# The norm's inverse root moved from eleven VectorE instructions to GpSimd's power, and taken per half in the first block

## The chip, the core and the metric

One NeuronCore of a Trainium2 chip runs the whole kernel. The metric is the device time of one execution in microseconds, given as the median over the runs of a kernel. Engines are named as in the profile: PE is TensorE (PEld its weight loads), DVE is VectorE, ACT is ScalarE, POOL is GpSimd, and SP is the engine that only issues transfers here.

## What is computed

The reference is an attention without softmax, a norm over the head dimension, and a gated feed-forward block:

```python
kv  = np.einsum('bhsd,bhse->bhde', k, v)          # 8 batches, 8 heads, 576 tokens, 64 wide
out = np.einsum('bhsd,bhde->bhse', q, kv)
rms = np.sqrt(np.mean(out * out, axis=-1, keepdims=True) + 1e-06)
x   = (out / rms * g_norm)                         # then (B,H,S,D) -> (4608, 512)
g   = x @ w_gate                                   # 512 -> 1536
silu = g * (1.0 / (1.0 + np.exp(-g)))
y   = (silu * (x @ w_val)) @ w_out                 # 1536 -> 512
```

The inputs reach the chip as 64-bit floats. Attention inputs are loaded through strided views, and the feed-forward weights are converted to float32 on the chip, from their two 32-bit words.

## The kernel before

The 4608 tokens are taken in nine blocks of 512 (`NB` = 9). A block has an attention part (class `Att`) and a feed-forward part (class `Ffn`). The attention part of block n + 1 is done inside the last stage of block n, so that TensorE always has products to work on. Block 0 has nobody to hide behind: its attention part is the method `first` (L466), and it is the start of the program.

The attention part of a block consists of these steps. `turn_q` transposes q. `heads` multiplies q with the kv matrix of each head into two PSUM tiles per half of the tokens. `squares` (L367) squares these tiles on ScalarE (L374) and sums them over the head dimension on VectorE (L375) into a small tile `z`: 128 partitions, and 32 values in each, 16 for each half of the tokens. `root` (L377) makes the inverse square root of the mean of squares plus epsilon. It does this on VectorE with one affine step (L381), a first guess from the bits of the number (L384) and three Newton steps of three instructions (L391 to L393): eleven instructions on 128x32 values. `scale` (L395) multiplies each PSUM tile with the root, broadcast over the head dimension, on VectorE (two instructions for each half, recorded at the helper's line L113). `turn_x` transposes the result on TensorE (L410), and ScalarE copies it with the gain (L411) to the tile `x`. From block 1 on, `whole` (L505) does both halves in one go, with one root for both, and the transposes are made by VectorE and transfers (`blocks_x`, `place_x`); `root` there is recorded after the second half's squares.

In `first`, both halves share one root as well: `heads` and `squares` of half 0, the products and squares of half 1, then `root(0, 2)`, `scale(0)`, the first weight piece, `turn_x(0)` and `scale(1)`. Between the products of half 1 and the transposes of half 0 stands `warm` (L492): seven float32 products of 128x512 that nobody reads, put in TensorE's queue.

Weights come in pieces of 512 KB. A piece is begun by `Words.begin` (ScalarE L146, then VectorE L147, L152 and L153) and finished by `Words.finish` (ScalarE L160, then VectorE L162). Block 0's feed-forward part (`plain_up`, L1032) needs one piece of `w_gate` and one of `w_val` for each of its 12 column groups; its first column group is split in two halves of the tokens, so that the first can begin when half 0 of x is there.

Three things order the work. Each engine has one queue and takes it in order. The program leaves the order to a scheduler, which follows priorities and the data; `tc.issue_after(...)` holds instructions back until another has been issued. Pools give the buffers: `st_pool` (two) for `z` and `y`, `r_pool` (five) for the large rings, PSUM pools `a` (one bank), `b` (three), `c` (two), `m` (two). GpSimd has no work until 105.78 us; later it has subtractions of weights (L112), some products and sums. Before each attention part of blocks 3 to 8 stand three subtractions of `turn_t(7)`, and three of `turn_t(4)` that wait for the scales (L1003).

Of the kernel before, what the change touches and what calls it, by code (L numbers as in the profile page):

```python
# [8 lines left out]
F32 = mybir.dt.float32  # L9
U32 = mybir.dt.uint32  # L10
I32 = mybir.dt.int32
OP = mybir.AluOpType
ACT = mybir.ActivationFunctionType

P = 128
# [3 lines left out]
def kernel(  # L19
# [41 lines left out]
    nc = tc.nc  # L61

    B, H, S, D = q.shape
# [7 lines left out]
    NS = DM // P  # L71
# [4 lines left out]
    eps = 1e-6  # L76
# [3 lines left out]
    def pool(name, bufs, **kw):  # L80
        return ctx.enter_context(tc.tile_pool(name=name, bufs=bufs, **kw))

    consts = pool("consts", 1)
    ld_pool = pool("ld", 4)
    st_pool = pool("st", 2)
# [8 lines left out]
    a_psum = pool("a_psum", 1, space=PS)  # L94
    b_psum = pool("b_psum", 3, space=PS)
# [6 lines left out]
    gain = consts.tile([P, 1], F32, name="gain")  # L102
    for u in range(2):
        nc.gpsimd.dma_start(out=gain[u * D : (u + 1) * D], in_=g_norm.rearrange("(d o) -> d o", o=1))

    kvs = [consts.tile([P, NS, D], F32, name=f"kv{i}") for i in range(3)]

# [11 lines left out]
    class Words:  # L119
# [12 lines left out]
        def __init__(self, src, shape):  # L132
            self.raw = ld_pool.tile([P, LD], U32, name="ld")[:, 0 : 2 * BLK]
            dst = self.raw.rearrange("p (a b) -> p a b", a=shape[0])
            self.sent = nc.sync.dma_start(out=dst, in_=src)
            self.shape = shape
            self.begun = False
# [45 lines left out]
    def round_w(name, j):  # L183
        if name == "o":
            dst = wo[:, j : j + 1, :]
        else:
            dst = wviews[name][0][j // 2][:, :, P * (j % 2) : P * (j % 2 + 1)]
        piece = words.pop((name, j))
        if not piece.begun:
            piece.begin()  # L190
        return piece.finish(dst)

    class Att:


        def __init__(self, n):
            self.n = n

            self.cut, half = divmod(n, 2)
            self.split = half * D  # L200
            self.ps, self.z = {}, None
            self.q, self.k, self.v, self.room = [], {}, {}, None
            self.halves = []
            self.quarters = n > 0

        def parts(self, t):

            n, first = self.n, P * t - D * self.n
            if t < self.cut:
                return [(n - 1, S + first, 0, P)]  # L210
            if t == self.cut and self.split:
                return [(n - 1, S - D, 0, D), (n, 0, D, P)]
            return [(n, first, 0, P)]
# [162 lines left out]

        def root(self, i, k=1):  # L377


            z = self.z[:, i : i + k]  # L380
            nc.vector.tensor_scalar(out=z, in0=z, scalar1=1.0 / D, scalar2=eps, op0=OP.mult, op1=OP.add)  # L381
            self.y, a = (st_pool.tile([P, 2, 2, 2, NS], F32, name=x) for x in "ya")
            y, a = self.y[:, i : i + k], a[:, i : i + k]
            nc.vector.tensor_scalar(  # L384
                out=y.bitcast(I32), in0=z.bitcast(I32), scalar1=-0.5, scalar2=float(0x5F3759DF),
                op0=OP.mult, op1=OP.add,
            )
            flat = lambda t: t.rearrange("p i u t j -> p (i u t j)")
            y, a, z = flat(y), flat(a), flat(z)
            for _ in range(3):  # L390
                nc.vector.scalar_tensor_tensor(out=a, in0=y, scalar=-0.5, in1=y, op0=OP.mult, op1=OP.mult)  # L391
                nc.vector.tensor_tensor(out=a, in0=a, in1=z, op=OP.mult)
                nc.vector.scalar_tensor_tensor(out=y, in0=a, scalar=1.5, in1=y, op0=OP.add, op1=OP.mult)  # L393

        def scale(self, i):  # L395
            if i == 0:
# [69 lines left out]
        def first(self):  # L466
            self.turn_q(0, (b_psum, c_psum))
            self.first_kv(0, (b_psum, c_psum))
            last = self.first_kv(1, (b_psum, a_psum))

            with tc.issue_after(last.ins):
                self.heads(0, (0, 1), (m_psum, m_psum))
            with tc.issue_after(self.multiplied.ins):
                self.heads(0, (2, 3))
            self.squares(0)
            with tc.issue_after(self.multiplied.ins):
                self.turn_q(1, (b_psum, c_psum))

            with tc.issue_after(self.copied_q.ins), tc.issue_after(self.summed.ins):
                begun = words[pieces[0]].begin()  # L480
            with tc.issue_after(begun.ins):
                self.product(1, (b_psum, a_psum))
            self.warm()
            self.root(0, 2)
            self.scale(0)
            with tc.issue_after(self.squared.ins), tc.issue_after(self.scaled.ins):
                weights(1)
            self.turn_x(0)
            self.scale(1)
            return self.squared, self.scaled  # L490

        def warm(self):  # L492

            ps = c_psum.tile([P, NS, P], F32, name="c")
            for _ in range(7):
                nc.tensor.matmul(ps, lhsT=ident, rhs=self.qt[:, 3], start=True, stop=True)

        def turn(self):
# [553 lines left out]
    def load_weights(upto):  # L1052
        nonlocal loaded, sent
        while loaded < min(upto, len(pieces)):
            load_w(*pieces[loaded])
            loaded += 1
            if loaded == len(pieces) - NP:
                sent = words[pieces[loaded - 1]].sent

    def weights(upto):  # L1060
        nonlocal rounded
        while rounded < min(upto, len(pieces)):
            load_weights(rounded + 4)
            round_w(*pieces[rounded])
            rounded += 1
# [106 lines left out]
```

## Time and profile before

| | |
|---|---|
| time, median of 3 runs | 1024.2 us (1023.02 to 1026.13) |
| span of the profiled execution | 1021.4 us |
| granted TensorE clock | 1.000 |
| first transposes of x (L410) | at 27.16 us |
| TensorE without gaps from | 33.72 us |
| one root on VectorE, block 0 | 2.47 us (23.26 to 25.73) |
| GpSimd's first instruction after the constants | at 105.78 us |

The profile is of one execution. A row of a timeline gives start, duration, engine, line of the kernel, operation, output<-inputs, shapes and count, and in brackets how long the engine had been idle before it and what it waited for. The page has the totals by engine, the busy share in 40 slices of the span (a digit is tenths), and the chain that ended last.

### The profile page before, as it was taken

Reading aid. Unit: us, or ns where it says so; the run is one execution under the profiler, and the core shown is the slowest. Engines: PE = TensorE matmul, PEld = TensorE weight load, DVE = VectorE, ACT = ScalarE, POOL = GpSimd, SP = SyncE. Lnnn points to the kernel's source line nnn. Section 1 sums busy time; section 2 is a strip of 40 time slices with the busy share of each in tenths; the row PEclk is TensorE's granted clock in tenths of the full one; section 3 lists DMA queues with packets and bytes.
Section 4 is the critical chain, followed back from the end, with each engine's and each line's share of the span. In section 5 each row is a group of like instructions: output and inputs, shape, how many; then the busy total and the mean of one; then the engine's idle time right before and its main releaser. Section 6 shows DMA issues by size and latency. Waiting matters only on the chain.

```text
span 1021.4 us, 21409 instructions
## 1 busy us (share of the span) xinstructions
PE 1006.0 (98%) x8522; PEld 897.1 (88%) x8522; DVE 701.1 (69%) x1169; ACT 227.9 (22%) x353; POOL 369.0 (36%) x280
## 2 busy tenths in 40 slices
PE   6999999999999999999999999999999999999998
PEld 4544688888999989998999899988998999989997
DVE  2999688998665946685558566665669466946661
ACT  2765112121211221121121211111121211221110
POOL 0000263534055503561246315630555045513670
PEclk9999999999999999999999999999999999999999
DMA  8689643767888377845686568636772766066601
GB/s 237 203 255 271 124 77 108 187 165 156 250 210 255 60 176 203 252 92 129 209 238 144 96 195 247 177 60 201 231 199 46 177 195 190 22 167 201 191 27 42
DMA packets 273845, 170.26 MB, mean 167 GB/s; under 512 B 150609, under 2 KB 241873, under 8 KB 273745
## 3 DMA queue, kind: packets, MB, share of 16 engines
q1 hardware_dynamic: 238800, 164.42, 59.3%
q10 hardware_dynamic: 34880, 4.46, 2.7%
q8 instruction: 68, 1.11, 0.4%
q14 instruction: 33, 0.26, 0.1%
q0 software_dynamic: 64, 0.00, 0.0%
HBM read 138.02 MB, written 22.41 MB: 157 GB/s over the span
## 4 chain that ended last, share of the span: by engine, by line
PE 90%; DVE 6%; DMA 2%; issue 1%; ACT 1%; SPq 0%; DVEq 0%; ACTq 0%
PE b L728 26%; PE b L565 19%; PE c L728 13%; PE c L565 10%; PE a L728 6%; PE a L565 5%; PE b L1032 4%; PE c L1032 4%; PE m L316 2%; PE m L361 1%; DVE r L112 1%; DVE xi L112 1%; DVE r L111 1%; DMA h<-in_v_dram 1%; DVE t L112 1%
## 5 line engine op out<-in xcount | busy, mean ns | idle before, releaser
L111 POOL TENSOR_TENSOR r<-r 128x256 f32<-128x256 f32 (+1 forms) x105 | 110.8, 1061 | 300.9 <-DVE r L111 272.2
L111 DVE TENSOR_TENSOR r<-b,r 128x512 f32<-128x512 f32 (+1 forms) x273 | 161.9, 606 | 65.5 <-PE b L728 60.1
L112 POOL TENSOR_TENSOR t<-wo 128x512 f32<-128x512 f32 x81 | 114.5, 1438 | 212.4 <-DVE wo L111 102.9
L111 DVE TENSOR_TENSOR r<-c,r 128x512 f32<-128x512 f32 (+1 forms) x179 | 108.5, 617 | 89.0 <-PE c L728 54.8
L728 PE MATMUL b<-x,t 128*128 128x128 f32 x1092 | 151.3, 276 | 0.0
L111 DVE TENSOR_TENSOR r<-a,r 128x512 f32<-128x512 f32 (+1 forms) x99 | 62.5, 631 | 113.4 <-PE a L565 70.7
L728 PEld LDWEIGHTS b<-x,t 128*128 128x128 f32 x1092 | 136.5, 192 | 0.8
L728 PE MATMUL c<-xi,t 128*128 128x128 f32 x840 | 112.4, 276 | 0.4 <-DVE xi L111 0.4
L113 POOL TENSOR_TENSOR h<-r 128x1024 f32<-128x1024 f32 (+1 forms) x40 | 82.3, 2072 | 76.9 <-DVE r L111 73.9
L728 PEld LDWEIGHTS c<-xi,t 128*128 128x128 f32 x840 | 102.9, 192 | 0.5 <-DVE xi L111 0.5
L565 PE MATMUL b<-wo,h 128*128 128x256 f32 x432 | 100.1, 383 | 0.1
L565 PE MATMUL b<-t,h 128*128 128x256 f32 x432 | 96.9, 381 | 0.0
L565 PEld LDWEIGHTS b<-t,h 128*128 128x128 f32 x432 | 81.6, 190 | 11.3 <-issue 0.2
L565 PEld LDWEIGHTS b<-wo,h 128*128 128x128 f32 x432 | 79.9, 190 | 13.1 <-DVE h L113 2.5
L742 ACT COPY r<-b 128x512 f32<-128x512 f32 x63 | 36.9, 585 | 211.6 <-PE b L728 211.6
L728 PE MATMUL b<-xi,t 128*128 128x128 f32 x588 | 79.8, 276 | 0.0
L728 PEld LDWEIGHTS b<-xi,t 128*128 128x128 f32 x588 | 72.4, 192 | 0.0
L728 PE MATMUL b<-x,wg 128*128 128x128 f32 x336 | 52.7, 279 | 0.2 <-DVE x L112 0.2
L728 PE MATMUL b<-x,wv 128*128 128x128 f32 x336 | 51.4, 276 | 0.0
L565 PE MATMUL a<-wo,h 128*128 128x256 f32 x216 | 48.3, 379 | 0.0
L565 PE MATMUL c<-t,s 128*128 128x256 f32 x216 | 48.1, 380 | 0.0
L565 PE MATMUL c<-wo,h 128*128 128x256 f32 x216 | 48.1, 379 | 0.0
(133 smaller groups left out, 1565.7 us busy)
## 6 DMA issues: line engine op xcount, KB each, us to landing
t<-w SPq DMA_DIRECT2D x336, 256.0 KB, 3.6
out_dram<-r SPq DMA_DIRECT2D x17, 512.0 KB, 3.1
ld<-in_k_dram SPq DMA_DIRECT2D x26, 288.0 KB, 5.2
ld<-in_v_dram SPq DMA_DIRECT2D x26, 288.0 KB, 5.9
ld<-in_moe_w_gate_dram SPq DMA_DIRECT2D x12, 512.0 KB, 4.8
ld<-in_moe_w_val_dram SPq DMA_DIRECT2D x12, 512.0 KB, 4.7
ld<-in_moe_w_out_dram SPq DMA_DIRECT2D x12, 512.0 KB, 4.9
w<-t SPq DMA_DIRECT2D x18, 256.0 KB, 3.0
```

The lines of the kernel that those rows point to most:

```text
L111: add = lambda e, o, a, b: e.tensor_tensor(out=o, in0=a, in1=b, op=OP.add)
L112: sub = lambda e, o, a, b: e.tensor_tensor(out=o, in0=a, in1=b, op=OP.subtract)
L113: mul = lambda e, o, a, b: e.tensor_tensor(out=o, in0=a, in1=b, op=OP.mult)
L316: nc.tensor.matmul(self.kv_ps[r][u * D : (u + 1) * D, g, :], lhsT=k[:, u, c, :], rhs=v[:, u, c, :], start=(c == 0), stop=(c == KT - 1),)
L361: self.multiplied = nc.tensor.matmul(self.ps[i][u][p : p + D, t, j, :], lhsT=self.qt[rows, 2 * i + t, j, p : p + D], rhs=kvs[b % 3][rows, ...
L565: nc.tensor.matmul(banks[e][:, e], lhsT=lhsT, rhs=rhs, start=first and i == 0 and (e == 0 or banks[0] is not banks[1]), stop=i == self.ste ...
L728: nc.tensor.matmul(ps[:, i, f], lhsT=self.weight(o, p, f), rhs=self.operand(o, p), start=first and (i, f) == (0, 0), stop=True, skip_group ...
L742: nc.scalar.copy(out=dst, in_=ps)
L1032: nc.tensor.matmul(t, lhsT=w[f // 2][:, i, P * (f % 2) : P * (f % 2 + 1)], rhs=x[:, i, of], start=(i == 0), stop=(i == NS - 1),)
```

## The change

The root is taken by GpSimd: one affine step and one power with the exponent -0.5 from a constant tile, in place of eleven instructions of VectorE, in all nine blocks. In block 0 each half of the tokens has a root of its own, so that half 0 can be scaled and transposed before half 1 is squared and summed; the beginning of the first weight piece is put between, and the squares of half 1 after the scale of half 0. The unused products go from seven to two. It is meant to take work off VectorE in the start of the program and to let TensorE begin with real work earlier.

```diff
+    half = consts.tile([P, 8 * NS], F32, name="half")
+    nc.gpsimd.memset(half, -0.5)
...
         def root(self, i, k=1):
-            z = self.z[:, i : i + k]
-            nc.vector.tensor_scalar(out=z, in0=z, scalar1=1.0 / D, scalar2=eps, op0=OP.mult, op1=OP.add)
-            self.y, a = (st_pool.tile([P, 2, 2, 2, NS], F32, name=x) for x in "ya")
-            y, a = self.y[:, i : i + k], a[:, i : i + k]
-            nc.vector.tensor_scalar(
-                out=y.bitcast(I32), in0=z.bitcast(I32), scalar1=-0.5, scalar2=float(0x5F3759DF),
-                op0=OP.mult, op1=OP.add,
-            )
-            flat = lambda t: t.rearrange("p i u t j -> p (i u t j)")
-            y, a, z = flat(y), flat(a), flat(z)
-            for _ in range(3):
-                nc.vector.scalar_tensor_tensor(out=a, in0=y, scalar=-0.5, in1=y, op0=OP.mult, op1=OP.mult)
-                nc.vector.tensor_tensor(out=a, in0=a, in1=z, op=OP.mult)
-                nc.vector.scalar_tensor_tensor(out=y, in0=a, scalar=1.5, in1=y, op0=OP.add, op1=OP.mult)
+            self.y = self.y or st_pool.tile([P, 2, 2, 2, NS], F32, name="y")
+            z, y = (x[:, i : i + k].rearrange("p i u t j -> p (i u t j)") for x in (self.z, self.y))
+            nc.gpsimd.tensor_scalar(out=z, in0=z, scalar1=1.0 / D, scalar2=eps, op0=OP.mult, op1=OP.add)
+            nc.gpsimd.tensor_tensor(out=y, in0=z, in1=half[:, 0 : 4 * NS * k], op=OP.pow)
...
             self.squares(0)
+            self.root(0)
             with tc.issue_after(self.multiplied.ins):
                 self.turn_q(1, (b_psum, c_psum))
 
             with tc.issue_after(self.copied_q.ins), tc.issue_after(self.summed.ins):
                 begun = words[pieces[0]].begin()
             with tc.issue_after(begun.ins):
-                self.product(1, (b_psum, a_psum))
+                self.scale(0)
+            first = self.scaled
+            with tc.issue_after(self.copied_q.ins):
+                self.heads(1, range(NS), (b_psum, a_psum))
             self.warm()
-            self.root(0, 2)
-            self.scale(0)
-            with tc.issue_after(self.squared.ins), tc.issue_after(self.scaled.ins):
+            with tc.issue_after(first.ins):
                 weights(1)
+                self.squares(1)
+            self.root(1)
             self.turn_x(0)
+            with tc.issue_after(self.squared.ins), tc.issue_after(self.summed.ins):
+                weights(2)
             self.scale(1)
             return self.squared, self.scaled
 
         def warm(self):
             ps = c_psum.tile([P, NS, P], F32, name="c")
-            for _ in range(7):
+            for _ in range(2):
                 nc.tensor.matmul(ps, lhsT=ident, rhs=self.qt[:, 3], start=True, stop=True)
```

More of the change, by code (lines that the diff above doesn't have):

```diff
@@ L200, in __init__ @@
             self.split = half * D
-            self.ps, self.z = {}, None
+            self.ps, self.z, self.y = {}, None, None
             self.q, self.k, self.v, self.room = [], {}, {}, None
```

## The prediction, made before the changed kernel was run

> **What bounds the kernel now.** I read the page first (engine totals, the 40 slices, the chain that ended last):
>
> ```profile
> PE 1006.0 (98%) x8522; PEld 897.1 (88%) x8522; DVE 701.1 (69%) x1169; ACT 227.9 (22%) x353; POOL 369.0 (36%) x280
> ...
> PE   6999999999999999999999999999999999999998
> ...
> PE 90%; DVE 6%; DMA 2%; issue 1%; ACT 1%; SPq 0%; DVEq 0%; ACTq 0%
> ```
>
> TensorE sets the end: it is full in every slice but the first, and 90% of the chain is its work. The waits of TensorE sum to 11.8 us, and 9.3 of them are for the first transfers. So time can only be gained where TensorE is busy with nothing useful, or cold. The timeline of TensorE between 20 and 36 us shows where (start, duration, engine, line; two records are one float32 matmul):
>
> ```profile
> 20.67 6.28 PE L496 MATMUL c<-r,ident 128*128 128x512 f32 x14
> 27.16 1.07 PE L410 MATMUL m<-ident,r 128*128 128x128 f32 x8 [0.21 <-DVE r L113]
> 28.57 1.99 PE L1032 MATMUL b<-x,wg 128*128 128x256 f32 x8 [0.34 <-ACT x L411]
> 30.40 0.93 PE L410 MATMUL m<-ident,r 128*128 128x128 f32 x7
> 31.41 1.99 PE L1032 MATMUL c<-x,wv 128*128 128x256 f32 x8
> 33.24 0.27 PE L410 MATMUL m<-ident,r 128*128 128x128 f32 x1
> 33.72 1.99 PE L1032 MATMUL b<-x,wg 128*128 128x256 f32 x8 [0.20 <-ACT x L411]
> ```
>
> The seven products of L496 are never read: they fill 20.67 to 26.95 while VectorE makes the root. From 33.72 on TensorE has no gap worth naming. VectorE in the same stretch (timeline of DVE):
>
> ```profile
> 21.96 1.27 DVE L375 TENSOR_REDUCE z<-r 128x8 f32<-128x512 f32 x2
> 23.26 0.18 DVE L381 TENSOR_SCALAR z<-z 128x32 f32<-128x32 f32 x1
> ...
> 25.50 0.19 DVE L393 SCALAR_TENSOR_TENSOR y<-a,y 128x32 f32<-128x32 f32 x1
> 25.73 1.29 DVE L113 TENSOR_TENSOR r<-m,y 128x512 f32<-128x512 f32 x2
> ...
> 28.13 0.68 DVE L113 TENSOR_TENSOR r<-a,y 128x512 f32<-128x512 f32 x1
> ...
> 30.67 0.68 DVE L162 CUSTOM_DVE_ANT_0 wv<-r 128x1024 uint16<-128x1024 uint16 x1
> ```
>
> VectorE has no gap from 18.75 to past 35 us: it bounds the start, and the root is 25.73 - 23.26 = 2.47 us of it. In later blocks the root stands elsewhere; block 3's, in the timelines of DVE and of POOL:
>
> ```profile
> 350.15 1.21 DVE L381 TENSOR_SCALAR z<-z 128x32 f32<-128x32 f32 x1
> ```
>
> ```profile
> 346.01 5.32 POOL L112 TENSOR_TENSOR t<-wo 128x512 f32<-128x512 f32 x3 [6.70 <-DVE h L112]
> ```
>
> L381 takes 1.21 us instead of 0.18 and ends just after GpSimd's subtractions do (351.33).
>
> **What the Trainium skill says.** *SBUF — State Buffer*, "SBUF: two separate sides": VectorE and GpSimd share one port pair, an exclusive lock for a whole instruction; a VectorE instruction in a two-port mode, or with two SBUF inputs, and one of GpSimd block each other. The trace agrees: 0.18 against 1.21 us above. *GPSIMD Engine Reference*, "2.1 Instruction dispatch": each instruction goes through a software dispatch, and the first call of a freshly loaded routine pays about 6 us that no instruction shows. No row here shows that. Same page, "7. Performance pitfalls for Q7 kernels": a dependent float32 chain costs 4 cycles a step. No row shows a power. *TensorE: Matmul & The Clock Gate*, "Part 1": after an idle window of about 3.4 us the array's clock halves. Here TensorE's records of 128x512 are as quick at 20.67 (6.28/14 = 0.45 us) as later (3.60/8), so it is warm.
>
> **The change part by part.**
>
> *Removed from VectorE:* 11 instructions, 2.47 us per block (3.5 where L381 is held). In block 0 this is on the path.
>
> *Added to GpSimd:* an affine step and a power, 128x16 twice in block 0, 128x32 once in each of blocks 1 to 8. GpSimd's float32 adds take 0.736 us for 128x256 and 2.36 for 128x1024 (groups by shape), so 2.1 ns an element and 0.2 us fixed: the affine step is 0.23 us. The power p has no row. Lower bound: the same 0.23. Upper: 0.2 + 16 elements of 100 cycles (an estimate: 25 dependent steps of the 4 cycles stated above, at the 1.2 GHz of that page's specifications) = 1.5 us. I take p = 0.5[...]. The memset of the constant (-0.5) is 0.1 us at 3 us, when GpSimd is idle. A wait between GpSimd and VectorE costs 0.09 us (DVE ends at 105.69, POOL starts 105.78).
>
> *Block 0 rebuilt.* The recorded order of the changed program on VectorE is: reductions of half 0, the three instructions that begin the first weight piece, scale of half 0, finish of the first piece, reductions of half 1, two instructions of the second piece, scale b, one instruction, scale a, finish of the second piece. Start to start a reduction, scale, finish or L153 takes 0.60, L147 and L152 0.335.
> - Reductions of half 0 end at 20.62 as now. ScalarE now does its unit copy (0.57) before the copy of the turned q and the magnitude, so L147 starts at 21.12 instead of 20.54.
> - The affine step ends at 21.2. L147 runs to 21.62. The power then holds the port against L153 (two SBUF inputs): L153 starts at 21.62 + p, the scale at 22.25 + p and ends at 23.5 + p. With p = 0.5: 24.0 instead of 27.02. What hides most of the wait is the begin of the piece, 1.27 us.
> - Finish and the reductions of half 1: the latter end at 25.33 + p. Queued behind the second root on VectorE are L147 and L152 (0.67), then scale b waits, and behind it everything for the weights. If the second power isn't disturbed, y is there at 25.83 + 2p; if it and L152 take turns on the port, 0.5 later. Scale b, L153, scale a: 1.85 us, so half 1 is scaled at 27.7 + 2p, or 28.3 + 2p.
> - TensorE: two unused products end at about 22.8; a pause of 1.3 us; the transposes of half 0 at 24.1 (now 27.16); the first half product 1.41 us later, until 27.4; then it waits for half 1. Five transposes 0.67, the wv product 1.83, three transposes 0.4, with 0.15 of lag: the second half of the first product starts at 30.9 + 2p or 31.35 + 2p, against 33.72. The gain is 2.85 - 2p or 2.4 - 2p: at p = 0.5, 1.9 or 1.4 us. With no clash at all it is 3.0 - p, 2.5 us. I take the middle, **1.9 us**.
>
> *Is it kept?* From 33.72 to 113 TensorE runs without a gap, weights finish ahead of use (the finish of wv for the second column at 35.45, used at 40.71), and VectorE, which sets the weights' pace (busy 10.0 of 10 us in the windows from 40 to 80), has the same lead. The q loads of block 1 follow from buffers that VectorE frees, so they come earlier too. Kept.
>
> *Blocks 1 to 8, at nothing.* GpSimd's queue has three subtractions ahead of the root (to 351.33), and three behind that wait for the scales anyway. Root there: 351.4 + 0.3 + about 0.8, so scales at 352.6 against 353.71. Who waits: the scales free PSUM bank a, wanted by TensorE at 362.93; even 9 us more would be hidden. The turned x goes by DMA until 367.88 and the first sums are wanted after 379: about 4 us spare.
>
> **The rivals.**
> - *Full gain.* p near its lower bound, no clash: 3.0 us, with luck a few tenths from VectorE's freed time at the block edges (TensorE waits 1.4 us on VectorE there in all): 1021.0. For it: the scheduler puts filler on VectorE right where it waits. Against: L147, L152 and L153 are just the instructions that block GpSimd, as L381 shows.
> - *The power is slow.* At p = 3, or with a first call of 6 us on one of the roots, block 0 loses 3.6 us: 1027.8. TensorE would then wait where it now multiplies for nothing. For it: no row of a power; two roots in series each enter the path. Against: GpSimd's other instructions cost near 2 ns an element. Beyond p of about 5 the later blocks would wait as well, and it would pass 1032.
> - *The clock.* With five products less TensorE pauses twice (1.3 and about 1.5 us); if that halves the clock for one window of 3.4 us, 1.7 us of the gain go: 1024.0. Against: no pause reaches the window.
>
> **How the numbers follow.** Likeliest, 0.42: 1024.2 - 1.9 = 1022.3. Full gain 0.31: 1021.0. Clock or other loss 0.07: 1024.0. Slow power 0.20: 1027.8 or more. The bound of 0.3% is 3.07 us, at the edge of the full gain; the times of before spread 3.1 us: faster 0.33, same 0.46, slower 0.21. Range: from 1020.2 (full gain and 0.8 for the spread) to 1028.0 (a power of 3 us); some 2 in 10 are outside, mostly slower.
>
> **What would show it.** A power row of 128x16 on POOL of 0.3 to 0.8 us; the transposes of half 0 near 24 us; scale b waiting for POOL; the second half of the first product near 32; TensorE without gaps after; in later blocks no wait on POOL. Wrong if the power is above 1.3 us, if VectorE's L147 to L153 stand still longer than p, or if TensorE's 256-column records near 25 us last longer than the 0.23 us apiece they take now.

## The result, and the profile after

The changed kernel took **1033.9 us** (median of 4 runs, 1033.08 to 1035.87), against 1023.68 for the kernel before in runs beside it (1023.02 to 1026.13): a ratio of 1.0096, 95% interval 1.0078 to 1.0113. It is 10 us slower, and outside the predicted range.

The page after: engine totals, TensorE's granted clock in 40 slices of the span (tenths), and the chain that ended last by engine.

```profile
PE 1006.1 (97%) x8512; PEld 896.6 (87%) x8512; DVE 680.6 (66%) x1070; ACT 227.8 (22%) x353; POOL 424.5 (41%) x301
...
PEclk9899999999999999999999999999999999999999
...
PE 65%; DVE 14%; DMA 7%; POOL 5%; issue 3%; SPq 3%; ACT 1%; ACTq 1%; POOLq 0%; DVEq 0%
```

The change did what it meant to VectorE: 701.1 us of work became 680.6. But TensorE's share of the chain fell from 90% to 65%: the rest of what ended last hung on other engines' work. Its clock shows an 8 in the second slice. GpSimd's busy time rose by 55.5 us. The groups of GpSimd with shapes kept apart (line, engine, operation, output<-inputs, shapes, count | busy us, mean ns | idle before) say what of:

```profile
L384 POOL TENSOR_TENSOR y<-z,half 128x32 f32<-128x32 f32 x8 | 43.5, 5438 | 0.7
L384 POOL TENSOR_TENSOR y<-z,half 128x16 f32<-128x16 f32 x2 | 5.9, 2945 | 0.2
```

A power of 16 values per partition takes 2.945 us, of 32 it takes 5.438: (5.438 - 2.945) / 16 = 0.156 us per value and 0.45 us fixed. The affine step beside it takes 0.22 to 0.31 us. The first two powers took 2.93 and 2.96 us, so a first call costs nothing extra. The eleven VectorE instructions had taken 2.47 us for 32 values.

Where TensorE waited (engine, line, what it waited for: us in total, times, longest):

```profile
PE m L401 <- DVE r L115: 4.6, 2, 2.3
...
PE b L562 <- ACT r L916: 3.7, 6, 1.4
PE m L363 <- DVE r L333: 1.9, 1, 1.9
PE b L725 <- DVE x L114: 1.3, 2, 0.6
```

Before, the first was 0.2 us, the last 0.2, and the other two weren't there. By windows, TensorE's idle time rose by 4.85 us in 0 to 40, by 2.0 in 120 to 240, and by 4.65 in 360 to 960 us: 11.5 in sum, the whole difference of the two spans (1032.9 - 1021.4). Its busy time is unchanged, 1006.1 against 1006.0, although five unused products are gone (6.28 us of them became 1.98). Of these 4.3 us, 3.0 are put back by two products of block 0 that were slow (3.40 and 3.61 us in place of 1.99 each, shown below). Some of the 4.85 us isn't the change's: the start-up transfers landed about 0.8 us later in this profile (the second group of q transposes at 18.72 us, 17.93 before).

**The start.** Timeline of VectorE:

```profile
22.76 0.69 DVE L155 SCALAR_TENSOR_TENSOR r<-r 128x512 uint32<-128x512 uint32 x1
25.19 1.29 DVE L115 TENSOR_TENSOR r<-m,y 128x512 f32<-128x512 f32 x2 [1.74 <-POOL y L384]
...
31.73 0.69 DVE L115 TENSOR_TENSOR r<-b,y 128x512 f32<-128x512 f32 x1 [2.79 <-POOL y L384]
```

The two scales (L115) stand in VectorE's queue waiting for the powers, 1.74 and 2.79 us, and everything for the weights stands behind them. The timeline of TensorE:

```profile
22.34 1.98 PE L493 MATMUL c<-r,ident 128*128 128x512 f32 x4
26.63 1.12 PE L401 MATMUL m<-ident,r 128*128 128x128 f32 x8 [2.31 <-DVE r L115]
28.03 3.40 PE L1029 MATMUL b<-x,wg 128*128 128x256 f32 x8 [0.29 <-ACT x L402]
33.77 0.78 PE L401 MATMUL m<-ident,r 128*128 128x128 f32 x5 [2.33 <-DVE r L115]
34.34 3.61 PE L1029 MATMUL c<-x,wv 128*128 128x256 f32 x8
...
38.12 2.07 PE L1029 MATMUL b<-x,wg 128*128 128x256 f32 x8
```

The transposes of half 0 start at 26.63, only 0.5 us before the 27.16 of the kernel before (1.3 without the later transfers), and the second half of the first product starts at 38.12 instead of 33.72. After the pause of 2.31 us the half product that took 1.99 us takes 3.40: the granted clock was 0.50 there, from about 27.5 to 30.9 us, and again from about 34.3 to 37.7.

**A later block.** Block 3 after: the sums and the scale on VectorE, the power, ScalarE's queue (ACTq is its issuing of transfers) and the product that waits:

```profile
353.32 2.46 DVE L377 TENSOR_REDUCE z<-r 128x8 f32<-128x512 f32 x4
...
357.38 5.44 POOL L384 TENSOR_TENSOR y<-z,half 128x32 f32<-128x32 f32 x1
362.85 0.69 DVE L115 TENSOR_TENSOR r<-m,y 128x512 f32<-128x512 f32 x1 [7.08 <-POOL y L384]
...
367.69 5.67 ACTq L425 DMA_DIRECT2D x<-r  x8
...
373.40 0.58 ACT L916 COPY r<-b 128x512 f32<-128x512 f32 x1 [14.38 <-DMA x<-r]
...
374.13 2.18 PE L562 MATMUL b<-t,h 128*128 128x256 f32 x9 [0.19 <-ACT r L916]
```

and the same places before:

```profile
348.84 1.27 DVE L375 TENSOR_REDUCE z<-r 128x8 f32<-128x512 f32 x2
...
353.71 0.69 DVE L113 TENSOR_TENSOR r<-m,y 128x512 f32<-128x512 f32 x1
...
358.56 5.89 ACTq L434 DMA_DIRECT2D x<-r  x8
...
364.49 0.58 ACT L919 COPY r<-b 128x512 f32<-128x512 f32 x1 [11.13 <-DMA x<-r]
...
368.93 2.43 PE L565 MATMUL b<-t,h 128*128 128x256 f32 x10
```

The scale comes 7.07 us after the sums (355.78 to 362.85), where it came 3.60 us after them before (350.11 to 353.71). Of the 7.07 us, 5.44 are the power; 1.3 pass at the start, until GpSimd has finished its subtractions (at 356.99); before, L381 waited for such subtractions too. Behind the scale stand the stream transposes, eight transfer issues in ScalarE's queue, and then, in the same queue, a copy of PSUM bank b (L916, L919 before) that has nothing to do with the norm. It starts as the last issue ends, at 373.36, although TensorE had filled the bank by 368.76. TensorE's fourth product of the block needs that bank. Before, the copy ended 368.93 - 365.07 = 3.9 us before it was needed; after, it ends as TensorE waits (0.19 us in this block, up to 1.4 in the others).

### The profile page after: what moved, and what is told of

Its sections match the earlier page's. It is cut to its first block, busy times and chain, and to the rows that moved or that the text cites. A ratio compares the mean times of both kernels' runs of the same rounds, so it can differ in the third digit from the quotient of the medians.

```text
span 1032.9 us, 21306 instructions
## 1 busy us (share of the span) xinstructions
PE 1006.1 (97%) x8512; PEld 896.6 (87%) x8512; DVE 680.6 (66%) x1070; ACT 227.8 (22%) x353; POOL 424.5 (41%) x301
## 4 chain that ended last, share of the span: by engine, by line
PE 65%; DVE 14%; DMA 7%; POOL 5%; issue 3%; SPq 3%; ACT 1%; ACTq 1%; POOLq 0%; DVEq 0%
PE b L725 26%; PE c L725 13%; PE b L562 10%; PE a L725 6%; PE c L562 6%; POOL y L384 4%; DMA x<-r 2%; PE a L562 2%; DMA ld<-in_moe_w_out_dram 2%; DVE r L115 2%; DVE h L115 2%; POOL t L114 2%; DVE r L411 1%; SPq L425 1%; DVE r L155 1%
## 5 line engine op out<-in xcount | busy, mean ns | idle before, releaser
L115 POOL TENSOR_TENSOR h<-r 128x1024 f32<-128x1024 f32 (+1 forms) x40 | 82.3, 2072 | 80.4 <-DVE r L113 77.0
L384 POOL TENSOR_TENSOR y<-z,half 128x32 f32<-128x32 f32 (+1 forms) x10 | 49.4, 4939 | 0.8
L115 DVE TENSOR_TENSOR r<-m,y 128x512 f32<-128x512 f32 x18 | 12.3, 686 | 55.9 <-POOL y L384 55.9
```

Of the source, the lines that this page charges most:

```text
L115: mul = lambda e, o, a, b: e.tensor_tensor(out=o, in0=a, in1=b, op=OP.mult)
L384: nc.gpsimd.tensor_tensor(out=y, in0=z, in1=half[:, 0 : 4 * NS * k], op=OP.pow)
```

## The experiments

Theory: the time is lost by the power's length, in two stages: in block 0 both roots stand on the path, and in the later blocks the late scale reaches TensorE through ScalarE's queue. Rivals: the regrouping of block 0 and TensorE's clock; the hand-over to GpSimd (its port, the order that the scheduler makes); another wait. Each kernel was timed beside the kernel before, whose median was 1023.84 to 1024.45 in these comparisons; ratios are to it, with their 95% intervals. Where a product stands in place of the power (three kernels), the root is left out there and only its time is looked at.

**The power without its length.** The root is left out in all blocks.

```diff
-            nc.gpsimd.tensor_tensor(out=y, in0=z, in1=half[:, 0 : 4 * NS * k], op=OP.pow)
+            nc.gpsimd.tensor_tensor(out=y, in0=z, in1=half[:, 0 : 4 * NS * k], op=OP.mult)
```

> The changed kernel with a product in place of each power (z times -0.5, so the root itself is left out and x has other values); order, waits and unused products stay. Theory (the length of the power is what costs: 2.94 us for 128x16, 5.44 for 128x32): the prediction's formula with p = 0.25 gives a gain of 1.9 to 2.8 us, so 1020.9 to 1021.8 us, TensorE with less than 0.5 us of waits in the later blocks, half 0's transposes near 23.5 us. Rival (the regrouping, the hop between engines or the clock with only two unused products is what costs): still above 1027 us.

Measured: 1018.84 us (1018.18 to 1022.26), ratio 0.9951 (0.9938 to 0.9963), clock 1.000. TensorE in the start:

```profile
24.38 1.06 PE L401 MATMUL m<-ident,r 128*128 128x128 f32 x8 [0.52 <-DVE r L115]
25.79 1.99 PE L1029 MATMUL b<-x,wg 128*128 128x256 f32 x8 [0.34 <-ACT x L402]
28.84 0.74 PE L401 MATMUL m<-ident,r 128*128 128x128 f32 x5 [1.06 <-DVE r L115]
...
31.50 2.07 PE L1029 MATMUL b<-x,wg 128*128 128x256 f32 x8
```

With the same order and the same two unused products, TensorE has no long pause, its clock stays, and the second half begins at 31.50, 6.6 us before the changed kernel and 2.2 before the kernel before. The whole loss of the change, and 5.6 us more, hangs on the power's length. That the gain is larger than the start's 2.2 us is taken up below.

**One stage at a time.** The power in block 0 alone (Newton steps in the later blocks), and in blocks 1 to 8 alone (block 0 as before):

```diff
         def root(self, i, k=1):
+            if self.n == 0:      # in the other kernel: self.n > 0, with the start of before
                 ...              # affine step and power on GpSimd
+            else:
+                ...              # the eleven VectorE instructions
```

> Power in block 0 only (with the regrouped start and two unused products); blocks 1 to 8 have the eleven VectorE instructions again. Theory (the start and the later blocks each pay about half): 1027.5 to 1030 us, TensorE's waits on ScalarE's copy before product 4 gone. Rival (the start alone): 1033 to 1034 us.

> The other part alone: power in blocks 1 to 8, block 0 as before with one Newton root and seven unused products. Theory: 4 to 5 us are lost at the block edges, 1028 to 1029 us, in some 0.5 to 1.4 us per block, in front of product 4 of the down projection (behind ScalarE's copy) and of the first products of the next block. Rival (as predicted, the later blocks hide it): 1023 to 1024.5 us.

Measured: block 0 alone 1030.27 us (1029.0 to 1030.34), ratio 1.0054 (1.0042 to 1.0066); later blocks alone 1029.51 us (1027.67 to 1030.38), ratio 1.0046 (1.0034 to 1.0058). That is 5.8 and 5.1 us, together 10.9, near the 10.2 of the whole change. The prediction had the later blocks at nothing. The waits stay with their stages: with block 0 alone the transposes of x wait (L419 in that kernel, 6.4 us in 2) and there is no wait for the copy; with the later blocks alone:

```profile
PE b L574 <- ACT r L928: 4.6, 6, 1.4
...
PE b L737 <- DVE x L114: 0.6, 1, 0.6
```

(the same copy and the same wait for x under that kernel's line numbers).

**More unused products, against the clock.** Four in place of two; then seven, and four more of 128x256 behind the first half product:

```diff
-            for _ in range(2):
+            for _ in range(4):          # second kernel: range(7)
                 nc.tensor.matmul(ps, lhsT=ident, rhs=self.qt[:, 3], start=True, stop=True)
...
+                if w is wg and halves == (0,):      # second kernel only
+                    for _ in range(4):
+                        nc.tensor.matmul(
+                            self.ps[f][1][:, 1:2], lhsT=w[0][:, 0, 0:P], rhs=x[:, 0, of], start=True, stop=True,
+                        )
```

> The changed kernel with four unused products in place of two, so that TensorE's pause before half 0's transposes shrinks from 2.3 us to some 0.5 us. Theory (the clock halves after the pause: the wv product of half 0 takes 3.6 us instead of 2.0, and that lies on the path): 1.5 to 2 us less than the changed kernel, 1032 us. Rival (only the wait for the power sets the start): as the changed kernel, 1033.9 us within 0.8.

> The changed kernel with TensorE kept busy in both pauses of block 0: seven unused products in place of two, and four more unused products of 128x256 behind the first half product. The order then also draws the wv product of the first half ahead of the transposes of the second half. Theory (part of block 0's loss is TensorE's clock, halved after pauses of 2.3 us): the three products that took 3.40, 3.61 and 2.07 us take 1.99 each, and the second half of the first product begins at about 35.2 us instead of 38.12: 1.6 us by the clock and 1.3 by the order, 1031.0 us. Rival (only the late root counts, and the clock falls anyway or recovers in the shade of a wait): the second half not before 37.5 us, 1033 us or more.

Measured: four, 1033.6 us (1032.3 to 1033.98), ratio 1.0084 (1.0071 to 1.0097), no gain that can be told from the changed kernel by the intervals; filled, 1031.72 us (1030.91 to 1033.11), ratio 1.0079 (1.0066 to 1.0092), clock 1.000. With four, the timeline of TensorE shows the pause and the fall of the clock moved on, not gone:

```profile
27.11 1.99 PE L1029 MATMUL b<-x,wg 128*128 128x256 f32 x8 [0.34 <-ACT x L402]
32.86 0.45 PE L401 MATMUL m<-ident,r 128*128 128x128 f32 x1 [3.75 <-DVE r L115]
33.36 3.78 PE L1029 MATMUL c<-x,wv 128*128 128x256 f32 x8
```

The first half product is quick, the wait for half 1 is longer by as much, and the next product is slow. With both pauses filled every product is quick, but the wv product now stands ahead of the transposes of half 1 and waits for its weights, which VectorE finishes only behind the late scales:

```profile
34.55 1.99 PE L1029 MATMUL c<-x,wv 128*128 128x256 f32 x8 [1.22 <-DVE wv L164]
...
37.76 1.99 PE L1029 MATMUL b<-x,wg 128*128 128x256 f32 x8 [0.34 <-ACT x L402]
```

The second half begins at 37.76 instead of the 35.2 expected. So the start came only 0.4 us earlier. The median is 2.2 us below that of the changed kernel, though the two intervals overlap; of the profiled spans' difference (1032.9 - 1031.3 = 1.6 us) most is block 1's wait for its turned q, 0.2 us instead of 1.9. The halved clock is real, but its two slow products (3.40 and 3.61 us) stretched over time in which TensorE would mostly have waited. The theory of 1.6 us by the clock isn't borne out as a gain; what the clock costs alone wasn't isolated.

**The regrouping without the power.** The changed order, each half's root by the eleven VectorE instructions:

```diff
-            nc.gpsimd.tensor_scalar(out=z, in0=z, scalar1=1.0 / D, scalar2=eps, op0=OP.mult, op1=OP.add)
-            nc.gpsimd.tensor_tensor(out=y, in0=z, in1=half[:, 0 : 4 * NS * k], op=OP.pow)
+            ...                         # affine step, first guess, three Newton steps on nc.vector, as before
```

> The changed kernel's order (a root for each half in block 0, two unused products), but each root again by the eleven VectorE instructions. Theory (the power's length lost the time, the regrouping did not): a root of 128x16 on VectorE takes 11 instructions of about 0.2 us, 2.2 us; against the run with a product in place of the power, whose second half began at 31.50 us, VectorE has two such roots more, up to 4.0 us, partly behind the begin of the first piece: the second half begins at 33.5 to 35.5 us (33.7 before), the later blocks keep the whole group of kv products that saved about 0.45 us each there. In sum 1020.5 to 1023.5 us. Rival (the regrouping itself costs, because TensorE pauses and its clock falls): second half later than 36 us and 1026 or more.

Measured: 1027.83 us (1027.3 to 1029.94), ratio 1.0037 (1.0024 to 1.005): the rival's side. VectorE's timeline shows why my estimate of two roots of 2.2 us, partly hidden, was too kind:

```profile
28.15 0.17 DVE L383 TENSOR_SCALAR z<-z 128x16 f32<-128x16 f32 x1
...
33.57 0.17 DVE L395 SCALAR_TENSOR_TENSOR y<-a,y 128x16 f32<-128x16 f32 x1
...
34.26 0.68 DVE L115 TENSOR_TENSOR r<-b,y 128x512 f32<-128x512 f32 x1
```

The second root (its first and last step, and the scale behind it) begins at 28.15 and ends at 33.7. The scheduler put another instruction, mostly one for the weights, between every two of its steps, so that eleven steps of 0.17 us took 5.6. The transposes of half 1 come at 35.69 (before, VectorE scaled half 1 from 27.53), the second half begins at 37.09, and TensorE's clock falls after that pause too (3.51 us for the product). The order of block 0 isn't bad in itself (the run without the power's length shows that), but it needs a root that is short for its half.

**What the power does to VectorE.** The kernel before, with powers of four widths on GpSimd behind the first root, where GpSimd is idle and VectorE has no gap, and two products; nobody reads them:

```diff
+    for n in (8, 16, 32, 64):
+        nc.gpsimd.tensor_tensor(out=po[:, 0:n], in0=pr[:, 0:n], in1=ex[:, 0:n], op=OP.pow)
+    for n in (16, 64):
+        nc.gpsimd.tensor_tensor(out=po[:, 0:n], in0=pr[:, 0:n], in1=ex[:, 0:n], op=OP.mult)
```

> The kernel before, with powers of 128x8, 128x16, 128x32 and 128x64 on GpSimd behind the first root, where GpSimd has no work, and two products of 128x16 and 128x64; nobody reads them. Theory (a power costs 0.44 us and 0.156 us an element, and does not hold the port): 1.7, 2.9, 5.4 and 10.4 us; products 0.2 and 0.3 us; VectorE's instructions under them last as before (scales 1.29 for two, finish 0.68), TensorE's second half begins at 33.7 us, 1023.5 to 1025 us. Rival (the port is locked for the whole of a power): VectorE's instructions with two SBUF inputs stand still for up to 10 us, and the time grows by more than 5 us.

Measured: 1023.87 us (1023.08 to 1026.37), ratio 0.9998 (0.999 to 1.0006). GpSimd's groups:

```profile
L1086 POOL TENSOR_TENSOR po<-pr,ex 128x64 f32<-128x64 f32 x1 | 10.6, 10647 | 0.1
L1086 POOL TENSOR_TENSOR po<-pr,ex 128x32 f32<-128x32 f32 x1 | 8.0, 7968 | 0.1
L1086 POOL TENSOR_TENSOR po<-pr,ex 128x16 f32<-128x16 f32 x1 | 2.9, 2921 | 0.1
L1088 POOL TENSOR_TENSOR po<-pr,ex 128x16 f32<-128x16 f32 x1 | 2.2, 2245 | 0.1
L1086 POOL TENSOR_TENSOR po<-pr,ex 128x8 f32<-128x8 f32 x1 | 1.7, 1667 | 0.1
```

Widths 8, 16 and 64 lie within 3% of 0.44 + 0.156 a value (1.69, 2.94, 10.4). The 7.97 us of width 32 don't, where the eight roots of that width agree on 5.44; and the product of 128x16 behind them took 2.25 us where 0.2 was expected (the one of 128x64 next took 0.32). Both are left open; spans on GpSimd are rough. What matters is VectorE: 23 us of powers lay under its stream, from 26.48 to 49.92 us, and its instructions lasted as before (L153 0.69, scales 1.29 for two, L162 0.68), with no time lost. No power held VectorE up, as the subtractions hold L381: in the kernel before it took 1.21 or 1.22 us in the six blocks where one ran beside it, each time ending within 0.05 us of that subtraction, and 0.18 us in the three blocks where none did.

**The same work on GpSimd, in short instructions.** Block 0 as before; in blocks 1 to 8 the affine step, the first guess and three Newton steps of four instructions on GpSimd:

```diff
+            for _ in range(3):
+                nc.gpsimd.tensor_tensor(out=a, in0=y, in1=y, op=OP.mult)
+                nc.gpsimd.tensor_tensor(out=a, in0=a, in1=z, op=OP.mult)
+                nc.gpsimd.tensor_scalar(out=a, in0=a, scalar1=-0.5, scalar2=1.5, op0=OP.mult, op1=OP.add)
+                nc.gpsimd.tensor_tensor(out=y, in0=a, in1=y, op=OP.mult)
```

> Block 0 as before; in blocks 1 to 8 the root on GpSimd, but by the affine step, the first guess and three Newton steps of four instructions (14 of 128x32) in place of the power. Theory (only the length of GpSimd's work between the reductions and the scale loses the time): 14 of about 0.22 us, 3.1 us, against 5.66 with the power; the scale comes about 3.5 us after the reductions as before (7.1 with the power); no wait for the copy before the fourth product, 1023 to 1025 us. Rival (giving the root to GpSimd at all costs, by its port or by the order that the scheduler makes of it): 1027 to 1030 us, as with the power in the later blocks alone (1029.5).

Measured: 1026.0 us (1023.84 to 1027.71), ratio 1.0015 (1.0009 to 1.0021), between the two expectations. The 14 instructions take 4.4 us in block 3 (352.41 to 356.79), less than the affine step and power (357.07 to 362.82, 5.75 us), and TensorE no longer waits for the copy. In its profile, of a run 1.5 us below its median, the later blocks are as long as before to 0.1 us; what the remaining 1.8 us are stays open.

**The copy behind the issues.** One line of the changed kernel, then the same line with the power in the later blocks alone, and in the kernel before:

```diff
-            nc.scalar.copy(out=u3, in_=self.ps["b"])
+            nc.vector.tensor_copy(out=u3, in_=self.ps["b"])
```

> The changed kernel, with one copy (of PSUM b into the piece of x2 before the fourth product, ScalarE's queue in the changed kernel) made by VectorE. Theory (in blocks 3 to 8 the late scale delays eight transfer issues on ScalarE's queue, and the copy stands behind them): the waits of TensorE for that copy (3.7 us in 6) go, some of it comes back as a wait for x in the next block; 1030 to 1032 us. Rival (what is late is the scale's own consumer, not the queue): the wait stays under another name, 1033.2 to 1034.5 us.

> Block 0 as before, the power in blocks 1 to 8, and the copy ahead of the fourth product made by VectorE instead of ScalarE. Theory (all that the power loses in the later blocks goes through that copy behind the transfer issues on ScalarE's queue, but for 0.6 us of waiting for x): 1024.3 to 1025.8 us, against 1029.5 without the move. Rival (a part is lost in other ways): 1027 us or more.

> The kernel before with only that copy moved to VectorE. Theory (before, the copy has some 4 us to spare, so its engine is of no account): 1023.6 to 1024.8 us, as before. Rival (the move is itself a gain, and what it brought in the changed kernel says nothing on the power): under 1022 us.

Measured: the changed kernel with it 1029.43 us (1028.18 to 1030.3), ratio 1.0046 (1.0033 to 1.006); later blocks alone with it 1026.19 us (1024.64 to 1028.73), ratio 1.0018 (1.0011 to 1.0025); the kernel before with it 1022.13 us (1019.87 to 1023.74), ratio 0.9978 (0.9972 to 0.9985). In the first, block 3's copy is done when its bank is filled, and the product doesn't wait:

```profile
369.01 0.69 DVE L916 COPY r<-b 128x512 f32<-128x512 f32 x1 [1.36 <-PE b L562]
...
373.92 4.26 PE L562 MATMUL b<-t,h 128*128 128x256 f32 x19
```

Against the kernel before, 10.2 us became 5.2, so it took back some 5 us. But the control fell against the theory: the move gains 2 us where the copy had time to spare. And the kernel with the power in the later blocks alone stays 4.06 us above that control, so that not everything goes through the copy. Hence two more.

**The later blocks without the power's length.** Block 0 as before, a product in place of the power in blocks 1 to 8, with the copy on ScalarE and on VectorE:

```diff
-                nc.gpsimd.tensor_tensor(out=y, in0=z, in1=half[:, 0 : 4 * NS * k], op=OP.pow)
+                nc.gpsimd.tensor_tensor(out=y, in0=z, in1=half[:, 0 : 4 * NS * k], op=OP.mult)
```

> Block 0 as before; in blocks 1 to 8 GpSimd's affine step and a product by the constant in place of the power (the root is left out there). The same engine and the same order of hands, only the power's 5.4 us becomes 0.25. Theory (in the later blocks the power's length alone loses the time, and with a quick root the changed order there saves what moving the copy saved in the kernel before, 2 us): 1021.5 to 1023 us, against 1029.5 with the power. Rival (handing the root to GpSimd costs by itself): 1024.5 us or more.

> As the kernel with the power in the later blocks and the copy on VectorE (1026.2), with the product in place of the power (the root is left out in blocks 1 to 8). Theory (the 4 us by which that kernel is above the kernel before with the same copy moved, 1022.1, are the power's length, through x and block 1's q): 1021.5 to 1023 us. Rival (they come from the order or from GpSimd's port): 1025 us or more.

Measured: 1021.05 us (1020.46 to 1023.69), ratio 0.9975 (0.9965 to 0.9985), and 1021.87 us (1020.91 to 1023.77), ratio 0.9981 (0.9974 to 0.9988). Four kernels then make a square. Taken each against the kernel before in runs beside it, the power's length costs 5.06 + 2.79 = 7.9 us with the copy on ScalarE, and 2.01 + 1.97 = 4.0 us with the copy on VectorE (by the intervals, good to some 1.6 and 1.0 us). About half of it goes through the copy in ScalarE's queue. Of the other half the waits of TensorE show a part (the kernel with the power and the copy moved; engine, line, what it waited for, total, times, longest):

```profile
PE m L363 <- DVE r L333: 1.7, 1, 1.7
PE b L737 <- DVE x L114: 1.5, 3, 0.6
```

x is late by up to 0.6 us a block, as the scale is late. The 1.7 us for block 1's turned q are less sure: the same wait is there without the power (1.3 us in the first of these two kernels) and absent in other runs, so it isn't shown to be the power's. The rest of the 4.0 us stays open.

The square also shows why the change's loss looked like only 5.1 us in the later blocks: the new order there gains 2 to 2.8 us at the same time. Of this, 1.3 us can be seen, as TensorE's own busy time. The groups of the kv products, the kernel before:

```profile
L316 PE MATMUL m<-ld 64*64 64x64 f32 x936 | 19.0, 223 | 0.0
```

and the changed kernel:

```profile
L318 PE MATMUL m<-ld 64*64 64x64 f32 x936 | 17.7, 221 | 0.0
```

Before, five of the groups of 72 small products stand in two bursts of 34 and 38 in TensorE's queue, 0.79 and 0.80 us; in the changed kernel, in those with a product in place of the power, and in the kernel before with the copy moved, they stand in one burst of 1.28 us. The busy time is 1.3 us less; the three blocks between 340 and 664 us are 107.2 to 107.5 us long in the kernel without the power's length, against 107.7 to 107.8. What changed for these products is the order which the scheduler comes to. Giving the root to GpSimd doesn't bring it by itself: with the Newton steps there the products still take 19.0 us.

**A version that beats both.** The changed order of block 0 wants a root that is short for half the tokens and leaves VectorE and the path quickly. *ScalarE: Activation LUTs*, "What it computes", of the Trainium skill advises VectorE's reciprocal followed by a square root on ScalarE. So: block 0 with that root, Newton steps in the later blocks; then with the copy on VectorE as well.

```diff
             if self.n == 0:
+                nc.vector.tensor_scalar(out=z, in0=z, scalar1=1.0 / D, scalar2=eps, op0=OP.mult, op1=OP.add)
+                nc.vector.reciprocal(out=z, in_=z)
+                nc.scalar.activation(out=y, in_=z, func=ACT.Sqrt)
...
-            nc.scalar.copy(out=u3, in_=self.ps["b"])            # second kernel only
+            nc.vector.tensor_copy(out=u3, in_=self.ps["b"])
```

> The changed kernel's order in block 0, but the root there by the affine step and a reciprocal on VectorE (128x16, about 0.2 us each) and a square root on ScalarE (about 0.3 us, and a table load of 1.28 us as the later one for Silu takes, put in ScalarE's queue ahead of it); blocks 1 to 8 with the Newton steps as before. Theory (the order of block 0 is good, once a root of one half takes about 1 us): half 0 scaled from about 23.5, half 1 from 29 us, the second half of the first product at 32 us, 1.5 us ahead of before; 1021.5 to 1023 us. Rival (the table loads stand in ScalarE's way, or the pauses halve the clock all the same): 1024 to 1027 us.

> The changed order of block 0 with the root there by affine step, reciprocal and ScalarE's square root, the Newton steps in the later blocks, and the copy ahead of the fourth product on VectorE. Theory (the two gains, 0.75 us in block 0 and 2.05 us by the copy, are of separate stages and add): 1020.8 to 1022 us, below both kernels. Rival (the later blocks take back what block 0 gains): 1022 to 1023.5 us.

Measured: 1023.43 us (1021.34 to 1028.4), ratio 0.9995 (0.9987 to 1.0003), not to be told from the kernel before; with the copy moved **1020.46 us** (1018.11 to 1020.53), ratio 0.9956 (0.9943 to 0.9969), below both kernels. ScalarE in the start of the first of them:

```profile
20.99 1.28 ACT L385 ACT_TABLE_LOAD   x1
22.29 0.22 ACT L385 ACTIVATE y<-z 128x16 f32<-128x16 f32 x1
...
27.71 1.28 ACT L1052 ACT_TABLE_LOAD   x1
```

A root is a reciprocal of 0.25 us and a square root of 0.22. The extra table load (1.28 us) runs beside VectorE's begin of the first piece, and VectorE waits 0.37 us for the first root; the second half begins at 31.79 us, and the clock stays at 1.000. In its profile TensorE's gain of 1.9 us at the second half is the 1.9 us of the spans (1019.5 against 1021.4), but the medians show 0.75, and the interval includes no change. The gains of the two edits add, 0.75 + 2.05 = 2.8 expected, 3.4 measured.

## Why the prediction was wrong

- **The power's duration** is the step that failed. "I take p = 0.5", with an upper bound of 1.5: it measured 2.945 us for 16 values. The upper bound was 100 cycles a value, 0.083 us; the trace has 0.156. The figure behind it, the 4 cycles a step of the Trainium skill's *GPSIMD Engine Reference*, "7. Performance pitfalls for Q7 kernels", was multiplied by a guess of 25 steps, and that product isn't a bound. "GpSimd's other instructions cost near 2 ns an element", the argument against the slow rival, said nothing on a power: it costs 156 for each value of a partition.
- **The wider power.** For the 32 values of the later blocks the working put "about 0.8", from the same guess; it took 5.44. The rival of the slow power named a single p for both shapes, though the power grows with the values per partition. Its last clause, "beyond p of about 5 the later blocks would wait as well, and it would pass 1032", came true as written; but the rival's time, worked out at p = 3 with nothing for the later blocks, was 1027.8, 6 us short.
- **Block 0.** 2.85 - 2p with p = 2.94 is a loss of 3.0 us; the second half began 4.4 us later, 3.6 of them without the later transfers. The mechanism, two roots in series on the path and TensorE waiting where it multiplied for nothing, was right, and so are the places named: scale m and scale b wait for GpSimd. In time, block 0 alone lost 5.8 us. Beyond the start's shift its profile shows a wait of 1.9 us for block 1's turned q, which "kept" didn't foresee for a loss; whether it is the power's is open, as said above.
- **The clash on the port.** "The power then holds the port against L153" did not happen: L155 (L153 before) took 0.69 us at 22.76, in the middle of a power, and 23 us of powers under VectorE's stream cost nothing. *SBUF — State Buffer*, "SBUF: two separate sides", has the pair locked for a whole instruction; the trace fits this beside the subtractions (1.21 us for L381) and not beside a power. The measurement decides.
- **The clock.** "No pause reaches the window": a pause of 2.31 us was enough for the 1.99 us product to take 3.40. *TensorE: Matmul & The Clock Gate*, "Part 1", gives an idle window of about 3.4 us; it isn't a safe margin here. Nor does the length of one pause decide: with the power in block 0 alone TensorE paused for 2.64 us before the same transposes, and the next product still took 1.99. What the fall cost beyond the wait is small or open, as filling the pauses showed.
- **Blocks 1 to 8 "at nothing"** is the other step that failed: they lost 5.1 us as the change stands, and 7.9 by the square. The working looked at PSUM bank a ("even 9 us more would be hidden") and at x. It did not look at what stands behind the turned x in ScalarE's queue: eight issues, and then the copy of bank b for the fourth product, with 3.9 us to spare. What is queued behind a late instruction was followed on VectorE and GpSimd only. Nor were the 4 us for x enough. ScalarE takes up the landed x of block 3 at 379.28 us instead of 367.88; 5.7 of these 11.4 us are the later start of the block, the other 5.7 the later scale and the transfers behind it, and a product then waits 0.64 us for x (at 388.12).
- **The order.** That the scheduler would order the kv products anew, worth 2 to 2.8 us, was in no term. Without it the change would have come out slower still, so that here luck hid a part of the loss.

## What to carry to other kernels

An operation without a row is not bounded by its neighbours: the power on GpSimd costs by the value, some 70 times what an add does (156 against 2.1 ns), and such a term deserves a chance as large as the ignorance. Before a step in a later stage is put at nothing, follow its result through every queue that it passes, transfer issues included: whatever stands behind them on that engine is delayed too, as the copy on ScalarE was here. And work taken off an engine that doesn't set the end need not bring anything: VectorE had 20 us less to do, and the kernel was 10 us slower. What counts is how long the step on the path takes, as the product in the power's place shows.

## What the runs showed of the hardware that was not expected

- A GpSimd power takes 0.156 us per value and partition and 0.44 fixed (1.67, 2.94, 5.44 and 10.65 us for 8, 16, 32 and 64 values, one record of 7.97 for 32 apart), and VectorE ran beside it undisturbed (L153 0.69 us, L162 0.68).
- TensorE's clock fell after a pause of 2.31 us, and the fall showed only after most of 1.1 us of transposes (26.63, then the slow product at 28.03 us). After 2.64 us, in another kernel, the next product was quick. Each of the two slow stretches of the changed kernel lasted 3.4 us.
- The same 936 small products take 19.0 or 17.7 us of TensorE by how they are grouped in its queue.
- A Newton root on GpSimd, 14 instructions of 0.22 to 0.25 us, was quicker for 32 values (4.4 us) than its power with the affine step (5.75).
- A ScalarE copy whose bank was full at 368.76 us started at 373.40, as the eight transfer issues ahead of it in the queue ended.
